# Keys and values streamed once: other pieces for the keys, other places for the weights

## The chip, the cores and the metric

The kernel runs on one core of one Trainium2 chip. The metric is the device time of one execution in microseconds (us). Before the change the median of three runs is 664.82 us (663.97 to 667.68). TensorE is called PE, VectorE DVE, ScalarE ACT, GpSimd POOL; SyncE (SP) here only issues DMAs, which run on the core's sixteen DMA engines.

## The reference

One decoding step of a transformer block, four sequences of one token each, 32 heads, 4096 cached positions, head size 128, model width 640. Attention and a gated MLP both start from the same normalised input and are added to it:

```python
q = (x @ wq).reshape(B, Sq, Hq, Dh).transpose(0, 2, 1, 3)
scores = jnp.einsum('bhqd,bhkd->bhqk', q, k) * Dh ** (-0.5)
o = jnp.einsum('bhqk,bhkd->bhqd', softmax(scores), v)
A = o.transpose(0, 2, 1, 3).reshape(B, Sq, Hq * Dh) @ wo

z = gelu(jnp.einsum('bsd,df->bsf', x, w_in))
z1, z2 = z[..., :Fh], layernorm(z[..., Fh:])
Bm = jnp.einsum('bsf,fd->bsd', z1 * (w_sp * z2 + b_sp), w_out)   # one position, so w_sp is a scalar
return x_in + A + Bm                                            # x = layernorm(x_in) in both
```

The two caches are 134 MB each in bfloat16, and every byte is used once. All else (wq, wo 5 MB each, w_in 2 MB, w_out 1 MB) is small beside them.

## The kernel before

**Units.** The work is cut into 16 units (`NU`), u = 4 * hg + b: a group `hg` of eight heads for one sequence `b`. The cached rows of a unit, 8 x 4096 of them, are laid over the 128 partitions ("lanes") so that each lane holds 256 consecutive rows: one contiguous run of 64 KB in memory for K(u), and another for V(u).

**Scores on DVE.** A K run is worked on in four quarters of 64 rows (16 KB a lane). For each quarter DVE multiplies by the query in place (`product`), adds the upper half of each row to the lower (`fold_half`), PE adds eight slices with an identity as weights (`sums`, eight matmuls into PSUM), and DVE sums the last eight values of each row (`row_sums`), one quarter later. After a unit's last quarter come `head_max`, `exps` on ACT and `by_head`, which writes the probabilities spread by head into the tile `pm` of that unit's parity. They stand inside the first quarter of the next unit. The weighted sum of V (`weighted`, 64 matmuls of PE) follows later, then a copy by ACT (`take`), and one quarter or more later a pick of the right blocks by PE (`pick_unit`, `pick_last`). At the end of a group, `group_turn` on DVE normalises and transposes and `group_proj` on PE multiplies with the group's 1.3 MB of `wo`, adding to the result in PSUM.

**Places.** SBUF holds three tiles of 32 KB a lane for K halves (`kp`, `K_SLOTS`), one of 64 KB for V (`vp`), and one of 10 KB for `wo` (`wop`). The first contents of the V tile are wq and w_in (`w_a`), of the `wo` tile w_out (`w_b`).

**Order of loads.** All large loads are issued by SP, in the order of the list `loads`: K halves 0 to 2, then for each unit its V and the next two K halves (three after units 3, 6, 9: `EXTRA_K`), then the last two units' V as four halves in K's places and V's. SP's queue is strictly in order: a load that waits for its place holds up all that stand behind it. `pump` lets loads into the program as soon as the user of their place is written down. The loop over the 32 halves is written out by hand (`manual_schedule`), so each engine keeps exactly that order. `turns` says after which half a V run's weighted sum stands. `gmlp`, the whole gated MLP, stands ahead of the loop.

Of the kernel before, what the change touches and what calls it, by code (L numbers as in the profile page):

```python
# [9 lines left out]
FP32 = mybir.dt.float32  # L10
# [4 lines left out]

K_SLOTS = 3
EXTRA_K = (3, 6, 9)
# [3 lines left out]
def kernel(  # L21
# [36 lines left out]
    NC = NR // 2  # L58
    HC = NC // 2
    NT = 2 * NU  # L60
    HD2 = Dh // 2
    RW = 8
    SLOT = NC * Dh
# [12 lines left out]
    kp = ctx.enter_context(tc.tile_pool(name="kp", bufs=K_SLOTS))  # L76
    vp = ctx.enter_context(tc.tile_pool(name="vp", bufs=1))
    wop = ctx.enter_context(tc.tile_pool(name="wop", bufs=1))
# [14 lines left out]

    w_a = vp.tile([P, 2 * SLOT], BF16, tag="v", name="w_a")
    wq_sb = w_a[:, 0 : DC * HD].rearrange("p (c n) -> p c n", c=DC)
    w_in_sb = w_a[:, DC * HD : DC * (HD + F)].rearrange("p (c n) -> p c n", c=DC)
    w_b = wop.tile([P, HT, D], BF16, tag="wo", name="w_b")
    w_out_sb = w_b[:, 0:NFC, :]
# [7 lines left out]
    nc.sync.dma_start(out=w_in_sb, in_=B_w_in.rearrange("(p c) n -> p c n", c=DC))  # L106
    nc.sync.dma_start(
        out=w_out_sb[:, 0:NFF, :], in_=B_w_out[0 : NFF * P].rearrange("(p k) n -> p k n", k=NFF)
    )
    nc.sync.dma_start(out=w_out_sb[:FT, NFF, :], in_=B_w_out[NFF * P : Fh])  # L110
# [7 lines left out]
    k_tiles, v_tiles = {}, {}  # L118
    V_CUTS = (0, 64, 96, 112, NC)

    def half_run(t, cache, i, cuts=(0, NC)):
        u, half = divmod(i, 2)
        for c0, c1 in zip(cuts, cuts[1:]):
            nc.sync.dma_start(
                out=t[:, c0 * Dh : c1 * Dh],
                in_=run_of(cache, u)[:, (half * NC + c0) * Dh : (half * NC + c1) * Dh],
            )
        return t[:, 0:SLOT].rearrange("p (c d) -> p c d", d=Dh)

    def load(which, n):  # L130
        if which == "k":
            k_tiles[n] = half_run(kp.tile([P, SLOT], BF16, tag="k", name="k_nat"), A_k_cache, n)
        elif which == "v":
            t = vp.tile([P, 2 * SLOT], BF16, tag="v", name="v_nat")
            nc.sync.dma_start(out=t[:], in_=run_of(A_v_cache, n))  # L135
            v_tiles[n] = t[:].rearrange("p (c d) -> p c d", d=Dh)
        elif which == "h":
            v_tiles["h", n] = half_run(
                kp.tile([P, SLOT], BF16, tag="k", name="v_half"), A_v_cache, n
            )  # L140
        else:
            t = vp.tile([P, 2 * SLOT], BF16, tag="v", name="v_end")[:, 0:SLOT]
            v_tiles["h", n] = half_run(t, A_v_cache, n, V_CUTS)

    loads = [("k", 0), ("k", 1), ("k", 2)]
    n_k = 3
    turns = {}
    for u in range(NU - 2):
        turns[n_k - 1] = u
        loads.append(("v", u))  # L150
        for _ in range(3 if u in EXTRA_K else 2):
            if n_k < NT:
                loads.append(("k", n_k))
                n_k += 1
    loads += [("h", NT - 4), ("h", NT - 3), ("h", NT - 2), ("e", NT - 1)]
    used = set()
    n_loaded = [0]
    holders = {"k": [], "v": [("w", 0)]}

    def pump():  # L160
        while n_loaded[0] < len(loads):
            which, n = loads[n_loaded[0]]
            ring, slots = (holders["v"], 1) if which in "ve" else (holders["k"], K_SLOTS)
            if len(ring) >= slots and ring[-slots] not in used:
                return
            load(which, n)
            ring.append((which, n))
            n_loaded[0] += 1

    wo_tiles = {}  # L170

    def load_wo(hg):
        wo_tiles[hg] = wop.tile([P, HT, D], BF16, tag="wo", name="wo")
        rows = A_wo[hg * HT * Dh : (hg + 1) * HT * Dh]
        if hg == HG - 1:
            by_head = rows.rearrange("(h p) n -> p h n", p=P)
            for h0, h1 in ((0, 2), (2, 4), (4, 6), (6, 7), (7, 8)):
                nc.sync.dma_start(out=wo_tiles[hg][:, h0:h1, :], in_=by_head[:, h0:h1, :])
            return
        nc.sync.dma_start(  # L180
            out=wo_tiles[hg][:].rearrange("p (e j) n -> p e j n", e=PAR),
            in_=rows.rearrange("(e p j) n -> p e j n", e=PAR, j=JR),
        )
# [20 lines left out]
    p_m = [const.tile([P, NG, CB, HT], BF16, name=f"pm{n}") for n in range(2)]  # L204
# [121 lines left out]
    def gmlp():  # L326
# [95 lines left out]
        for k in range(NFC):  # L422
            w = P if k < NFF else FT
            for half in range(2):
                nc.tensor.matmul(
                    out=out_sum(half),
                    lhsT=gm["yT"][:w, k, :],
                    rhs=w_out_sb[:w, k, half * NOH : (half + 1) * NOH],
                    start=False,
                    stop=False,  # L430
                )
# [18 lines left out]
    def half_of(i, half):  # L450
        return k_tiles[i][:, half * HC : (half + 1) * HC, :]

    def product(i, half):
        nc.vector.tensor_tensor(  # L454
            out=half_of(i, half),
            in0=half_of(i, half),
            in1=qbcs[i // 2][:, None, :].to_broadcast([P, HC, Dh]),
            op=ALU.mult,
        )

    def fold_half(i, half):
        t = half_of(i, half)
        nc.vector.tensor_tensor(  # L463
            out=t[:, :, 0:HD2], in0=t[:, :, 0:HD2], in1=t[:, :, HD2:Dh], op=ALU.add
        )

    def sums(i, half):
        t = half_of(i, half)
        s = sums_ps[i, half] = ps_s.tile([P, HC, RW], FP32, name="s_ps")
        n = HD2 // RW  # L470
        for g in range(n):
            nc.tensor.matmul(  # L472
                out=s[:],
                lhsT=ident[:],
                rhs=t[:, :, g * RW : (g + 1) * RW],
                start=(g == 0),
                stop=(g == n - 1),
            )

    def row_sums(i, half):  # L480
        u, which = divmod(i, 2)
        if (which, half) == (0, 0):
            scores[u] = small.tile([P, NR], FP32, name="s_sb")
        at = which * NC + half * HC
        nc.vector.tensor_reduce(  # L485
            out=scores[u][:, at : at + HC], in_=sums_ps.pop((i, half))[:], axis=AX.X, op=ALU.add
        )
# [25 lines left out]
    def by_head(u):  # L513
        hg, b = divmod(u, Bsz)
        nc.vector.tensor_tensor(  # L515
            out=p_m[u % 2][:],
# [16 lines left out]
    def weighted(u, v_at, g0=0, more=False):  # L533
# [3 lines left out]
        for n in range(n_g):  # L537
# [3 lines left out]
                lhsT=p_m[u % 2][:, g0 + n].rearrange("p c h -> p (c h)"),  # L541
# [55 lines left out]
    def group_proj(hg):  # L597
        for n, o in enumerate(gr.pop(hg)):
            for half in range(2):
# [3 lines left out]
                    rhs=wo_tiles[hg][:, n, half * NOH : (half + 1) * NOH],  # L603
                    start=False,
                    stop=(hg == HG - 1 and n == HT - 1),
                )

# [18 lines left out]

    E = mybir.EngineType
    with tc.manual_schedule(engines={E.PE, E.DVE, E.Activation, E.SP}):
        stage_q(0)
        gmlp()  # L630
        used.add(("w", 0))
        pump()
        for i in range(NT):
            u, half = divmod(i, 2)
            due, done = turns.get(i), turns.get(i - 1)
            closed = None
            if done is not None and done % Bsz == Bsz - 1 and done // Bsz < HG - 1:
                closed = done // Bsz
            product(i, 0)
            if i:  # L640
                row_sums(i - 1, 1)
            if half == 0 and u:
                head_max(u - 1)
            if done is not None:
                picked(done)
            fold_half(i, 0)
            if half == 0 and u:
                exps(u - 1)
                by_head(u - 1)
            sums(i, 0)  # L650
            if closed is not None:
                group_turn(closed)
            if half == 0 and u + 1 < NU:
                stage_q(u + 1)
            product(i, 1)
            row_sums(i, 0)
            fold_half(i, 1)
            sums(i, 1)
            if closed is not None:
                group_proj(closed)  # L660
            if due is not None:
                if due % Bsz == Bsz - 1:
                    group_den(due // Bsz)
                weighted(due, v_tiles[due])
                take(due)
                used.add(("v", due))
            used.add(("k", i))
            pump()
            if i % (2 * Bsz) == 6 and i // (2 * Bsz) < HG - 1:
                load_wo(i // (2 * Bsz))  # L670
        load_wo(HG - 1)
        row_sums(NT - 1, 1)
# [3 lines left out]
        picked(NU - 3)  # L676
# [10 lines left out]
        weighted(NU - 2, v_tiles["h", NT - 4], more=True)  # L687
        weighted(NU - 2, v_tiles["h", NT - 3], NG // 2)
        take(NU - 2)
        for n in (NT - 4, NT - 3):  # L690
            used.add(("h", n))
        picked(NU - 2)
        u, b = NU - 1, Bsz - 1
        weighted(u, v_tiles["h", NT - 2])
        take(u)
        pick_last(u, more=True)
        for c in range(NC):
            nc.tensor.matmul(  # L698
                out=o_last[0][:, :, :, b],
                lhsT=v_tiles["h", NT - 1][:, c, :],  # L700
                rhs=p_m[u % 2][:, NG // 2 + c // CB, c % CB, :].rearrange("p (e k) -> p k e", e=PAR),
# [43 lines left out]
```

## Time and profile before

| | |
|---|---|
| median of three runs | 664.82 us |
| the profiled execution's own time | 663.56 us |
| its span, first to last instruction | 661.8 us |
| bytes loaded | 282.24 MB, 426 GB/s over the span |
| DVE busy | 522.4 us (79%) |
| PE busy | 328.9 us (50%) |
| ACT busy | 29.7 us (4%) |

A row of a group of instructions gives its line, engine and operation, what it writes and reads, the count, the busy time and the mean in ns. "Idle before" is time in which the engine stood still ahead of these, with what released it. Matmuls are pipelined, so a matmul's duration is longer than its share of a series: eight of `sums` take 3.57 us together, though one is shown with 0.6. A DMA's "time to landing" runs from its issue on SP to the semaphore that says it has arrived, and so holds the time that it stands in the queue behind earlier loads. The DMA share is the mean busy share of the sixteen DMA engines in a stretch.

### The profile page before, as it was taken

Reading aid. Unit: us, or ns where it says so; the run is one execution under the profiler, and the core shown is the slowest. Engines: PE = TensorE matmul, PEld = TensorE weight load, DVE = VectorE, ACT = ScalarE, POOL = GpSimd, SP = SyncE. Lnnn points to the kernel's source line nnn. Section 1 sums busy time; section 2 is a strip of 40 time slices with the busy share of each in tenths; the row PEclk is TensorE's granted clock in tenths of the full one; section 3 lists DMA queues with packets and bytes.
Section 4 is the critical chain, followed back from the end, with each engine's and each line's share of the span. In section 5 each row is a group of like instructions: output and inputs, shape, how many; then the busy total and the mean of one; then the engine's idle time right before and its main releaser. Section 6 shows DMA issues by size and latency. Waiting matters only on the chain.

```text
span 661.8 us, 4641 instructions
## 1 busy us (share of the span) xinstructions
PE 328.9 (50%) x1999; PEld 131.6 (20%) x1999; DVE 522.4 (79%) x325; ACT 29.7 (4%) x73; POOL 2.7 (0%) x12
## 2 busy tenths in 40 slices
PE   0625363645454555454635354644446455354656
PEld 0311121212121112121211121212112122121223
DVE  2399899695969998959599899696996978969600
ACT  0200000000000000000000000000000000000000
POOL 1000000000000000000000000000000000000000
PEclk9767686767756678577755686777566557776866
DMA  9999999999999999999999999999999999999996
GB/s 368 432 442 434 422 443 420 453 420 422 451 406 446 460 402 455 418 442 436 423 431 436 426 435 424 460 412 425 452 407 448 458 404 453 414 443 440 418 424 278
DMA packets 10144, 282.54 MB, mean 427 GB/s; under 512 B 1056, under 2 KB 2188, under 8 KB 3340
## 3 DMA queue, kind: packets, MB, share of 16 engines
q1 hardware_dynamic: 10104, 282.25, 99.1%
q8 instruction: 15, 0.25, 0.1%
q14 instruction: 5, 0.04, 0.0%
q10 hardware_dynamic: 20, 0.01, 0.0%
HBM read 282.24 MB, written 0.01 MB: 426 GB/s over the span
## 4 chain that ended last, share of the span: by engine, by line
DMA 50%; DVE 39%; PE 9%; issue 1%; SPq 1%; ACT 0%; DVEq 0%
DMA k_nat<-in_A_k_cache_dram 42%; DVE k_nat L454 22%; DVE k_nat L463 11%; PE s_ps L472 5%; DMA v_half<-in_A_v_cache_dram 4%; PE pv L539 4%; DMA wo<-in_A_wo_dram 3%; DVE pm L515 3%; DVE s_sb L485 2%; DVE m L491 1%; DVE mt L493 0%; SPq L135 0%; DVE mt L496 0%; DVE o_n L582 0%; PE out_ps L600 0%
## 5 line engine op out<-in xcount | busy, mean ns | idle before, releaser
L472 PE MATMUL s_ps<-k_nat,ident 128*128 128x512 bf16 x512 | 219.0, 605 | 286.8 <-DVE k_nat L463 286.8
L454 DVE TENSOR_TENSOR k_nat<-k_nat,qbc 128x8192 bf16<-128x8192 bf16 x64 | 282.7, 4416 | 75.4 <-DMA k_nat<-in_A_k_cache_dram 75.4
L472 PEld LDWEIGHTS <-ident 128*128 128x128 bf16 x512 | 70.9, 138 | 417.5 <-issue 412.7
L463 DVE TENSOR_TENSOR k_nat<-k_nat 128x4096 bf16<-128x4096 bf16 x64 | 145.9, 2280 | 0.0
L539 PE MATMUL pv<-v_nat,pm 128*32 128x512 bf16 x896 | 56.2, 408 | 0.0
L485 DVE TENSOR_REDUCE s_sb<-s_ps 128x64 f32<-128x512 f32 x64 | 43.6, 681 | 3.3 <-PE s_ps L472 3.3
L515 DVE TENSOR_TENSOR pm<-p_c,own 128x2048 bf16<-128x2048 bf16 x16 | 36.6, 2284 | 2.9 <-ACT p_c L504 2.9
L539 PEld LDWEIGHTS <-pm 128*32 128x32 bf16 x992 | 27.0, 106 | 45.8 <-issue 22.1
L551 ACT COPY o_rows<-pv 128x512 f32<-128x512 f32 x16 | 9.4, 586 | 308.4 <-PE pv L539 308.4
L706 DVE TENSOR_TENSOR o_n_last<-o_last,rden_all 128x32 bf16<-128x32 f32 x1 | 0.2, 191 | 25.4 <-PE o_last L698 25.4
L570 PE MATMUL o_ps<-o_rows,pick 128*128 128x128 f32 x96 | 13.9, 288 | 8.8 <-ACT o_rows L551 8.8
L504 ACT ACTIVATE p_c<-s_sb,nm 128x256 bf16<-128x256 f32 x16 | 8.1, 508 | 197.2 <-DVE nm L498 197.2
L570 PEld LDWEIGHTS o_ps<-o_rows,pick 128*128 128x128 f32 x96 | 11.6, 191 | 14.7 <-ACT o_rows L551 14.7
L539 PE MATMUL pv<-v_half,pm 128*32 128x512 bf16 x96 | 10.6, 618 | 6.7 <-DMA v_half<-in_A_v_cache_dram 6.7
L257 DVE TENSOR_SCALAR q_rows<-q_ps 128x512 bf16<-128x512 f32 x2 | 1.4, 690 | 14.4 <-PE q_ps L249 14.4
L249 PE MATMUL q_ps<-w_a,xnT 128*32 128x512 bf16 x40 | 4.5, 630 | 11.1 <-DMA w_a<-in_A_wq_dram 11.1
L448 ACT CAST qbc<-qbc_ps 128x128 bf16<-128x128 f32 x16 | 4.3, 266 | 107.4 <-PE qbc_ps L440 107.4
L491 DVE TENSOR_REDUCE m<-s_sb 128x1 f32<-128x256 f32 x16 | 6.7, 420 | 0.6
L440 PE MATMUL qbc_ps<-q_rows,of_row 128*128 128x128 bf16 x32 | 6.3, 286 | 0.6 <-DVE q_rows L257 0.6
L440 PEld LDWEIGHTS <-of_row 128*128 128x128 bf16 x32 | 4.3, 138 | 8.6 <-issue 8.2
L616 PE MATMUL o_last<-hot,o_rows 128*128 128x8 f32 x32 | 4.2, 259 | 3.0 <-ACT o_rows L551 3.0
L616 PEld LDWEIGHTS o_last<-hot,o_rows 128*128 128x128 f32 x32 | 3.9, 191 | 5.5 <-ACT o_rows L551 5.5
(86 smaller groups left out, 70.3 us busy)
## 6 DMA issues: line engine op xcount, KB each, us to landing
k_nat<-in_A_k_cache_dram SPq DMA_DIRECT2D x32, 4096.0 KB, 33.1
v_half<-in_A_v_cache_dram SPq DMA_DIRECT2D x3, 4096.0 KB, 27.4
w_a<-in_A_wq_dram SPq DMA_DIRECT2D x1, 5120.0 KB, 15.4
wo<-in_A_wo_dram SPq DMA_DIRECT2D x3, 1280.0 KB, 35.3
w_a<-in_B_w_in_dram SPq DMA_DIRECT2D x1, 2160.0 KB
v_end<-in_A_v_cache_dram SPq DMA_DIRECT2D x1, 2048.0 KB
v_end<-in_A_v_cache_dram SPq DMA_DIRECT2D x1, 1024.0 KB
v_end<-in_A_v_cache_dram SPq DMA_DIRECT2D x2, 512.0 KB, 28.0
```

The lines of the kernel that those rows point to most:

```text
L440: nc.tensor.matmul(out=qb_ps[:], lhsT=of_row[:, e, b].rearrange("p k f l -> p (k f l)"), rhs=q_rows[e][:, hg, :], start=(e == 0), stop=(e ...
L454: nc.vector.tensor_tensor(out=half_of(i, half), in0=half_of(i, half), in1=qbcs[i // 2][:, None, :].to_broadcast([P, HC, Dh]), op=ALU.mult,)
L463: nc.vector.tensor_tensor(out=t[:, :, 0:HD2], in0=t[:, :, 0:HD2], in1=t[:, :, HD2:Dh], op=ALU.add)
L472: nc.tensor.matmul(out=s[:], lhsT=ident[:], rhs=t[:, :, g * RW : (g + 1) * RW], start=(g == 0), stop=(g == n - 1),)
L485: nc.vector.tensor_reduce(out=scores[u][:, at : at + HC], in_=sums_ps.pop((i, half))[:], axis=AX.X, op=ALU.add)
L491: nc.vector.tensor_reduce(out=m1[:], in_=scores[u][:], axis=AX.X, op=ALU.max)
L504: nc.scalar.activation(out=p_c[u][:], in_=scores.pop(u)[:], func=ACT.Exp, bias=maxes.pop(u)[:], scale=1.0, accum_out=row_den[hg % NACC][:, ...
L515: nc.vector.tensor_tensor(out=p_m[u % 2][:], in0=p_c.pop(u)[:].rearrange("p (g c) -> p g c", c=CB)[:, :, :, None].to_broadcast([P, NG, CB, HT]
L539: nc.tensor.matmul(out=pvs[u][cg * QD : (cg + 1) * QD, :], lhsT=p_m[u % 2][:, g0 + n].rearrange("p c h -> p (c h)"), rhs=v_at[:, n * CB : ...
L551: nc.scalar.copy(out=o[:].rearrange("p c d -> p (c d)"), in_=pvs.pop(u)[:])
L570: nc.tensor.matmul(out=gr[hg][:], lhsT=pick[:, c, Bsz - 1 - b : P + Bsz - 1 - b], rhs=o[:, c, :], start=(b == 0 and c == 0), stop=(b == Bs ...
L616: nc.tensor.matmul(out=o_last[0][:, :, :, u % Bsz], lhsT=o[:, c, :], rhs=hot[:, c, :].rearrange("p (e k) -> p k e", e=PAR), start=(c == 0) ...
```

## The change

K(u) is loaded as one run of 64 KB a lane. K's places become one ring tile of seven quarter places of 16 KB (`k_ring`). Even units lie in places 3 to 6 and odd ones in 0 to 3, so two neighbours share place 3. The even unit has its first quarter there and the odd one its last, and the odd unit works on that quarter first (`k_order`). So K(u+2) may be issued when all of unit u and the first quarter of unit u+1 are done, that is, one unit ahead. Units 0, 14 and 15 are loaded in halves, the last two into other places. V's tile stays; V(14) is now loaded into it as one run, and V(15) in two parts into places 0 to 3.

`wo` has no tile of its own any more: each group's lies in place 6, the last quarter of an even unit, and its load stands in the one list, behind the K that follows the group's last V. Place 6 is given back by `group_proj`, now one quarter after `group_turn`. w_out is loaded into the probabilities' tile (`p_m`, one tile for both parities), its last 96 rows into V's tile behind w_in. The first half of K(0) is loaded ahead of w_in and w_out, and `gmlp` stands after the second quarter of the loop instead of ahead of it. The loop runs over 64 quarters.

```diff
-K_SLOTS = 3
-EXTRA_K = (3, 6, 9)
...
+    NK = 4
+    HC = NR // NK
+    NC = 2 * HC
...
+    QW = HC * Dh
+    RING = 2 * NK - 1
...
+    ring = places.tile([P, RING, QW], BF16, name="k_ring")
+    v_all = places.tile([P, NK * QW], BF16, name="v_all")
+    p_m = const.tile([P, 2, NG, CB, HT], BF16, name="p_m")
...
+    k_at, k_order = {}, {}
+    for u in range(NU):
+        k_at[u] = [r if u % 2 else NK - 1 + r for r in range(NK)]
+        k_order[u] = [NK - 1, 0, 1, 2] if u % 2 else [0, 1, 2, 3]
+    k_at[NU - 2], k_order[NU - 2] = [4, 5, 0, 1], [0, 1, 2, 3]
+    k_at[NU - 1], k_order[NU - 1] = [2, 3, 4, 5], [0, 1, 2, 3]
+    VE_AT, WO_AT = (0, 2), 6
+
+    def k_load(u, r0=0, r1=NK):
+        at = k_at[u][r0:r1]
+
+        def go():
             nc.sync.dma_start(
+                out=ring[:, at[0] : at[0] + r1 - r0, :],
+                in_=run_of(A_k_cache, u)[:, r0 * QW : r1 * QW].rearrange("p (r w) -> p r w", w=QW),
             )
+
+        return go, at
...
-    loads = [("k", 0), ("k", 1), ("k", 2)]
...
-    for u in range(NU - 2):
-        turns[n_k - 1] = u
-        loads.append(("v", u))
-        for _ in range(3 if u in EXTRA_K else 2):
-            if n_k < NT:
-                loads.append(("k", n_k))
-                n_k += 1
-    loads += [("h", NT - 4), ("h", NT - 3), ("h", NT - 2), ("e", NT - 1)]
+    loads = [k_load(0, 0, 2), (load_w, []), k_load(0, 2, 4), k_load(1)]
+    for u in range(NU - 4):
+        loads += [v_load(u), k_load(u + 2)]
+        if u % Bsz == Bsz - 1:
+            loads.append(wo_load(u // Bsz))
+    assert u + 2 == NU - 3
+    loads += [k_load(NU - 2, 0, 2), v_load(NU - 4), k_load(NU - 2, 2, 4), k_load(NU - 1, 0, 2)]
+    loads += [v_load(NU - 3), k_load(NU - 1, 2, 4), v_load(NU - 2)]
+    loads += [ve_load(0, (0, NC)), ve_load(1, V_CUTS), wo_load(HG - 1)]
+    busy = {V}
...
     def pump():
         while n_loaded[0] < len(loads):
+            go, at = loads[n_loaded[0]]
+            if busy.intersection(at):
                 return
+            go()
+            busy.update(at)
             n_loaded[0] += 1
...
+    turns = {NK * (u + 1) + 2: u for u in range(NU - 4)}
+    turns[NK * (NU - 3) + 3] = NU - 4
+    turns[NK * (NU - 2) + 3] = NU - 3
...
+        for n in range(NK * NU):
+            u, i = divmod(n, NK)
+            product(n)
+            if n:
+                row_sums(n - 1)
+            if i == 0 and u:
                 head_max(u - 1)
+                if waiting is not None:
+                    picked(waiting)
+                    if waiting % Bsz == Bsz - 1 and waiting // Bsz < HG - 1:
+                        closed = waiting // Bsz
+                    waiting = None
+            fold_half(n)
+            if i == 0 and u:
                 exps(u - 1)
                 by_head(u - 1)
+            sums(n)
             if closed is not None:
+                if i == 0:
+                    group_turn(closed)
+                else:
+                    group_proj(closed)
+                    closed = None
+            if i == 0 and u + 1 < NU:
                 stage_q(u + 1)
+            if n == 1:
+                gmlp()
+                busy.remove(V)
+            if n in turns:
+                w = waiting = turns[n]
+                if w % Bsz == Bsz - 1:
+                    group_den(w // Bsz)
+                weighted(w, v_runs)
+                take(w)
+                busy.remove(V)
             pump()
```

`sums(n)` gives back its quarter's place (`busy.remove(k_at[u][r])`) and `group_proj` place 6 (`busy.remove(WO_AT)`). Behind the loop, the last two units' weighted sums and the last group's projection stand as before.

## The prediction

> **What bounds the kernel now.** I read the page from the top first: which engine is full, in every slice.
>
> ```profile
> span 661.8 us, 4641 instructions
> PE 328.9 (50%) x1999; PEld 131.6 (20%) x1999; DVE 522.4 (79%) x325; ACT 29.7 (4%) x73; POOL 2.7 (0%) x12
> DMA  9999999999999999999999999999999999999996
> q1 hardware_dynamic: 10104, 282.25, 99.1%
> ```
>
> No engine is full, but the sixteen DMA engines are: the load queue's packets fill 99.1% of the span. Then the busy time by stretch (the last two columns are DMA share and GB/s), to see whether that holds inside the loop:
>
> ```profile
> 34.00:110.00 76.00, 35.76 (x150) 13.17 (x151) 72.63 (x37) 3.87 (x9) 0.00 (x0) 0.66 1.00 433
> 110.00:300.00 190.00, 96.17 (x543) 37.00 (x543) 158.00 (x89) 7.00 (x19) 0.00 (x0) 0.68 1.00 433
> 300.00:600.00 300.00, 150.68 (x816) 58.29 (x815) 259.76 (x146) 11.05 (x31) 0.00 (x0) 0.66 1.00 433
> ```
>
> The share is 1.00 and the rate 433 GB/s everywhere, at the group ends too. So a 64 KB run a lane (8.39 MB) takes 19.4 us, half of it 9.7, a unit (K and V) 38.75. The chain of waits names DVE for 39% of the span, but only because it follows a load back to the work that freed its place; the load then stood in a queue. How long, the issues with their time to landing show (last column, median us):
>
> ```profile
> k_nat<-in_A_k_cache_dram SPq DMA_DIRECT2D x32, 4096.0 KB, 33.1
> v_nat<-in_A_v_cache_dram SPq DMA_DIRECT2D x14, 26.4
> wo<-in_A_wo_dram SPq DMA_DIRECT2D x3, 1280.0 KB, 35.3
> ```
>
> A K half is issued 33.1 - 9.7 = 23.4 us before its own transfer begins, a V run 26.4 - 19.4 = 7.0 us (22.7 - 19.4 = 3.3 for the shortest landing of a V tile). This lead is what the change can spend: while it is positive nothing else matters; when it is negative, every microsecond is added to the end. To price it I need the pace of DVE and PE within a unit, from the chain in order of time and from the timeline at a group's end:
>
> ```profile
> 136.06 4.33 DVE k_nat L454
> 140.40 0.61 DVE s_sb L485
> ...
> 141.03 0.43 DVE m L491
> ...
> 142.14 2.20 DVE k_nat L463
> 144.34 2.20 DVE pm L515
> 146.54 4.33 DVE k_nat L454
> ...
> 153.73 3.57 PE s_ps L472 x8
> ```
>
> ```profile
> 206.51 0.77 DVE L582 TENSOR_SCALAR o_n<-o_ps,rden 128x128 bf16<-128x128 f32 x1
> 207.31 0.31 DVE L590 STREAM_TRANSPOSE o_t<-o_n 128x128 bf16<-128x128 bf16 x1
> 214.78 3.57 PE L472 MATMUL s_ps<-k_nat,ident 128*128 128x512 bf16 x8 [4.83 <-DVE k_nat L463]
> 218.28 1.45 PE L600 MATMUL out_ps<-wo,o_t 128*4 128x320 bf16 x16
> 218.38 0.33 SPq L124 DMA_DIRECT2D k_nat<-in_A_k_cache_dram  x1
> ```
>
> A quarter costs DVE 4.33 + 0.60 + 2.20 = 7.13 us, the first of a unit 10.48 (136.06 to 146.54, softmax of the unit before included), a unit 31.87; it fits into 38.75. The sums of a quarter take PE 3.57 us, the weighted sum of a V run 3.6 to 4.6, a group's projection 1.4 (until 219.73), its turn on DVE 1.2 (206.3 to 207.55).
>
> **The change, part by part.** Every engine keeps its instructions (DVE 325), but SP issues 52 DMAs instead of 66.
>
> *Longer runs.* 13 units' K come as one DMA. Gain: GB/s over share in pure K stretches is 433/1.01 (25 to 50 us) and 434/1.01 (113 to 128), in V stretches 445/1.03 (55 to 69) and 454/1.05 (95 to 108): 429 to 432, 0.6%. On 13 x 8.39 MB (252 us) that is 1.5 us; shares have two digits, so 0 to -2.5. I take -1.0. The V rows exclude a loss: such runs already go at full rate.
>
> The fixed part of each issue is hidden in these rows: three K halves issued together land 9.7 us apart. The Trainium skill ("DMA: Bandwidth & Descriptors", the two cost components under the anatomy of one DMA) prices a DMA at about 2.0 us plus bytes at 436 GB/s, so 14 fewer would be worth 28 us; the share of 1.00 disagrees.
>
> *Steady units.* Count from the landing of K(u+1), with V(u)'s transfer just begun. K(u+2) needs all of unit u and the first quarter of u+1, the shared place: 4.33 + 0.61 + 1.04 (maximum) + 2.20, then 3.57 of sums: issued at 11.8; its turn is at 19.4. V(u+1) needs the third quarter, then weighted(u): 10.48 + 2 x 7.13 + 3.57 + 4.4 = 32.7; its turn is at 38.75. From issue to first data on an empty queue I take 1.0 us, as at the start (first issue at 0.74, no data in the first microsecond, 456 GB/s in the second), the nearest row, as it too is a long load; the upper end is 2.5, what the small last write takes in all (issued at 659.29, span's end 661.8). Leads of 6.6 and 5.0: cost nothing. They replace leads of 23 and 7, so what stands behind SP's waits counts now.
>
> *wo in place 6.* wo(0) stands on SP's queue ahead of V(4), and waits for the last quarter of unit 4, the last user of place 6: 31.87 on DVE; then PE has weighted(3) (until 33) and the sums (1.9 warm to 3.57), so 35 to 36.9, with 1.0 to data 38 at most, against 38.75. V(4) is still in time: nothing, up to 1 us if late.
>
> K(6) is not. It needs place 6 back, so it waits for the projection that reads wo, one quarter after the group's turn. From the landing of K(5): 10.48 + 1.2 (turn) + 7.13 + 3.57 + 1.4 + 0.1 (semaphore, issue) + 1.0 = 24.9 us. Ahead of it lie only wo and V(4): 3.5 + 19.4 = 22.9 (wo's 1280-byte pieces run at some 380 GB/s, as in the tail's 383 and 404). The queue is dry for 2.0 us; if the engines end apart, their mean waits longer: in the last three microseconds of loads the share is 0.87, 0.55, 0.26, so the mean ends 1.3 us before the last: 3.3. I take 2.7. It happens after groups 0 and 1: 5.4. After group 2 nothing waits for place 6, as units 14 and 15 do not use it. DVE cannot give it back: the lost time is DMA time.
>
> The page of the Trainium skill named above speaks against the change here: with its fixed 2.0 us where I have 1.0, each dry spell would be 1 us longer, an estimate of 7.4 for both.
>
> *The front.* K(0)'s first half now lands at 16.1 (wq) + 9.7 = 26 instead of 34.5; that gains nothing, the bytes ahead of the end are the same. gmlp now stands between quarters 1 and 2: PE 3.5 and DVE's chain 6.0 (25.1 to 31.1), during which DVE works on nothing else. Quarter 4 starts at 67, 4 us after K(1) lands (16.1 + 9.7 + 8 of weights + 9.7 + 19.4 = 63). V(1) is issued at 67 + 24.7 + 3.6 + 4.4 = 100, with data at 101, against 102. Bounds 0 and +2; I take +0.3. w_out in the probabilities' tile is read long before its first writer: nothing.
>
> *The tail.* Before, V(13) was loaded after the last K; now K(15)'s second half comes after V(13). Behind the landing of K(13) stand six runs and two wo: 53 MB, 122.3 us, and 1.33 of the last projection as before: 123.6. DVE and PE need in that time: three units and a turn, 95.6 + 1.2; twice 0.9, as exp now stands behind the copy of a weighted sum on ACT; from the last fold to weighted(14) 9 to 11 (618.8 to 629.8 before, 2 of it that copy); weighted(14) 3.6 warm to 7.2 cold; half of V(15) 1.8 to 3.6; two copies and picks of 1.7; the last 128 matmuls 4.0; normalising and projection 3.1. Sum 123.5 to 130.9: 0 to +7 over the loads. PE comes almost straight from sums and warms up (64 took 4.4 from cold sums at 83.9), so near the low end: +1.5. This cover did not matter before.
>
> **Sum:** -1.0 + 0 + 5.4 + 0.3 + 1.5 = +6.2. The profiled execution took 663.56 (span 661.8 and 1.8 around it): 669.8. It is 1.26 under the median of the three runs (664.82), so against that median: 671.0.
>
> **Rivals.**
> - *No dry spell (not slower).* Between cold and warm PE lie 1.7 us for eight sums (3.57 at 214.78, 1.89 at 387.41). If quarter 5's sums run warm, K(6)'s chain is 23.2 and the spell 0.3; with a covered tail -1.0 + 0.6 + 0.3 = 0: 664.7. It decides when the chain from K(5)'s landing to issue comes under 21.9. Against it: PE is idle for 3.5 us before those sums, and cold there in the rows above. 0.14.
> - *More waits of the same kind.* wo's own issue late (+1 each), a restart of 2 us, within its bounds (+1 each), the front +2, the tail +5 cold: -1 + 2 x (3.3 + 2) + 2 + 5 = 16.6 at most, 681; half of these extras gives 676. For it: PE's granted clock of 0.66 to 0.68. Against: steady leads of 5 us absorb each alone. 0.21.
> - *Fewer issues pay (faster).* If each of the 14 issues left a gap, the share could hide 0.5% of 566 us, 2.8 us over some 45 transfers: 0.9 us for 14; with -2.5 for runs, no dry spells and a covered tail, 661.4. The skill's 2.0 us each, above, would make it 637. Against it: the share, and a K(6) that must wait. 0.03.
>
> **How the numbers follow.** The likeliest (0.62) is 671, with its own range 667.5 to 674.5. Down to 666.5 leaves out most of the first and third rival, up to 677.5 a quarter of the second: 0.2 in all. A measurement of this kernel can tell about 0.5%, 3.3 us. Slower by more: nearly all of the likeliest and all of the second, 0.81. Within: the first and the low edge of the likeliest, 0.16. Faster: 0.03.
>
> **What would show it.** Two dips of the DMA share, at about 240 and 400 us, of 2 to 4 us each, just before K issues released by the projection; K issues of 64 KB a lane landing about 26 us after issue (19.4 and the lead of 6.6); DVE waiting for K 5 to 8 us in every unit; the last loads ending about 4 to 6 us later. I am wrong if the share stays 1.00 through both group ends, if dips come in every unit (then a steady lead is mis-sized), or if the loads end in time and the end still moves (then it is the tail).

## The result and the profile after

The changed kernel takes 679.27 us (median of six runs, 678.63 to 680.39) beside 663.75 us for the kernel before on the same chip. The ratio is 1.0226, with a 95% interval from 1.0203 to 1.0249: slower by 2.3%. The forecast was 671.0 with a range that ended at 677.5, so the direction was right and the size was not: the change costs about 15.5 us, where 6.2 had been worked out. Of the four executions of the first try with the MLP moved forward, two (688.07 and 698.82 us) fell into a slower state of the chip and are left out of its ratio below.

The profiled execution took 679.59 us, its span is 677.8 us. These are the lines of the page that answer to those of before, with the group of the scores' products added (last columns: busy time and mean ns, then the idle time before them and what ended it):

```profile
span 677.8 us, 4614 instructions
PE 303.5 (45%) x1999; PEld 128.0 (19%) x1999; DVE 522.5 (77%) x325; ACT 29.6 (4%) x73; POOL 2.7 (0%) x12
DMA  9999999999999979999999989999999999999995
q1 hardware_dynamic: 8088, 282.24, 97.3%
L481 DVE TENSOR_TENSOR k_ring<-k_ring,qbc 128x8192 bf16<-128x8192 bf16 x64 | 282.7, 4417 | 98.1 <-DMA k_ring<-in_A_k_cache_dram 98.1
```

DVE's work is unchanged to a tenth of a microsecond (522.4 before). What changed is the row of the DMA engines: it is no longer full in two slices inside the loop. Each slice is 16.9 us, so the 7 stands at 237 to 254 us and the 8 at 390 to 407; the last slice, where the loads end, is a 5 and was a 6. The queue's share times the span gives the time that the packets took: 97.3% of 677.8 is 659.5 us, against 99.1% of 661.8, 655.8. So of the 16.0 us that the span grew, 12.3 are time in which the DMA engines had nothing to do, and 3.7 are packets that took longer. The same bytes moved.

The busy time by stretch, for the same three stretches as before (last two columns: DMA share and GB/s), says how much of it lies inside the loop:

```profile
34.00:110.00 76.00, 37.16 (x226) 16.33 (x224) 62.16 (x54) 6.88 (x13) 0.00 (x0) 0.59 1.00 427
110.00:300.00 190.00, 86.23 (x540) 35.48 (x540) 153.58 (x83) 6.67 (x18) 0.00 (x0) 0.68 0.98 422
300.00:600.00 300.00, 130.07 (x801) 54.09 (x801) 244.34 (x139) 10.94 (x31) 0.00 (x0) 0.68 0.99 424
```

Where it was 433 GB/s throughout, each stretch now has less. The first loses 6 of 433 with a full share, so its packets were slower. Now the end of the first group in fine steps, same columns. A packet is counted where it starts, and one of 64 KB takes some 2.4 us, so short steps scatter, but three microseconds without data are a gap:

```profile
236.00:241.00 5.00, 1.43 (x4) 0.55 (x4) 5.00 (x4) 0.00 (x0) 0.00 (x0) 0.53 0.97 419
241.00:244.00 3.00, 3.00 (x20) 1.06 (x19) 3.00 (x2) 0.00 (x0) 0.00 (x0) 0.64 0.00 0
244.00:246.00 2.00, 0.35 (x6) 0.10 (x1) 2.00 (x2) 0.00 (x0) 0.00 (x0) 1.00 1.55 524
```

The chain of waits in order of time (start, us, what) names the work that filled this gap:

```profile
193.90 26.54 DMA k_ring<-in_A_k_cache_dram
220.53 4.42 DVE k_ring L481
...
228.91 2.20 DVE p_m L542
231.29 0.78 DVE o_n L609
...
239.57 3.57 PE s_ps L496 x8
243.14 1.23 PE out_ps L627 x16
244.38 21.82 DMA k_ring<-in_A_k_cache_dram
...
357.51 26.49 DMA k_ring<-in_A_k_cache_dram
...
406.70 1.37 PE out_ps L627 x16
408.08 22.93 DMA k_ring<-in_A_k_cache_dram
```

K(5) lands at 193.90 + 26.54 = 220.44. DVE then does the first quarter, the turn of the group and the second quarter, PE the sums and the projection (L627), and K(6) is issued at 244.38: 23.94 us after the landing. K(10), likewise, is issued at 408.08, 24.1 after the landing of K(9) at 384.0. No such step stands in the chain after the third group.

How the queue starts again, the stretch from 243 to 246 us shows in 40 steps of 0.075 us (its rate, then its packets, MB and share):

```profile
GB/s 0 0 0 0 0 0 0 0 0 0 0 0 0 0 0 0 0 0 0 0 0 0 0 0 0 0 0 0 0 0 0 4369 2621 1748 874 1748 874 874 0 874
q1 hardware_dynamic: 16, 1.05, 103.1%
```

The first data comes in the 32nd step, at 245.3, 1.0 us after K(6)'s issue. Sixteen packets of 64 KB start, one for each engine; together they take 103.1% of 16 x 3 us, so 3.1 us each, where such a packet takes 2.42 in a full queue. The trace gives the other end, too: the engines had finished V(4) one by one between 241.1 and 242.8, at 241.5 in the mean, and its landing was told at 243.07. So an engine stood still for 4.0 us in the mean, of which the late issue is 1.3 (243.07 to 244.38). At K(10) it was 3.5 us, with 0.7 of late issue.

The issues of the load queue, with their median time to landing, show the steady units:

```profile
k_ring<-in_A_k_cache_dram SPq DMA_DIRECT2D x13, 26.7
v_all<-in_A_v_cache_dram SPq DMA_DIRECT2D x15, 26.2
```

19.4 us of a K's 26.7 are its own transfer, so it is issued 7.3 us before its turn ("turn" is the landing of the load ahead, and "lead" the time from an issue to it).

Last, the tail, in the timeline (start, us, engine and line, operation; in brackets the idle time before it and its releaser):

```profile
618.91 5.16 PE L566 MATMUL pv<-v_all,p_m 128*32 128x512 bf16 x64 [2.43 <-DMA v_all<-in_A_v_cache_dram]
624.17 0.59 ACT L578 COPY o_rows<-pv 128x512 f32<-128x512 f32 x1 [32.23 <-PE pv L566]
624.66 0.51 ACT L531 ACTIVATE p_c<-s_sb,nm 128x256 bf16<-128x256 f32 x1
625.29 2.29 DVE L542 TENSOR_TENSOR p_m<-p_c,own 128x2048 bf16<-128x2048 bf16 x1 [4.16 <-ACT p_c L531]
...
657.39 0.63 PE L705 MATMUL den_all<-acc,ones_sq 128*128 128x32 f32 x2 [5.05 <-DVE acc L551]
657.95 6.11 PE L566 MATMUL pv<-v_all,p_m 128*32 128x512 bf16 x64
```

The weighted sum of unit 13 waits for V(13) to land and then takes 5.16 us; ACT copies its result before it computes the probabilities of unit 14, and DVE stands still for 4.16 us. From here to the end, the chain runs on DVE and PE, with short pieces of ACT, and no longer on loads. In it the weighted sum of unit 14 takes 6.11 us, after PE had stood idle for 5.05.

**Where the 16.0 us are.** The landings in the trace split them. A load that is never late lands 19.3 us after the one ahead (a half 9.65, `wo` 3.05).

| | later by, us |
|---|---|
| K(6): lands at 266.20, V(4) ahead of it at 243.07; 23.1 | 3.8 |
| V(5) behind it: lands at 287.21; 21.0 | 1.7 |
| K(10): lands at 431.01, V(8) ahead of it at 407.38; 23.6 | 4.3 |
| front: K(2), then V(1) (82.36, 102.92, 123.76; 20.6 and 20.8) | 1.3 + 1.5 |
| second half of K(14) | 0.8 |
| `wo` of the first two groups, issued 3.5 and 3.3 us before their turn (3.2 and 3.8) | 0.9 |
| K(1) | 0.4 |
| all other loads, less the 3.8 us by which loads came late in the kernel before | -2.0 |
| last load to the end of the span: 3.4 before, 6.7 after | 3.3 |
| sum | 16.0 |

V(5) was issued 12.4 us before its turn and is late all the same. It belongs to the spell: the engines, which had ended V(4) 1.7 us apart, restart together and end K(6) 0.6 us apart, and by V(5) the slowest is 1.8 us behind the first again. V(5) is 1.0 to 1.7 us late in each of the five profiles with a spell at K(6), and in time in the kernels below that have none. So the two spells cost 5.5 and 4.3 us (5.54 and 4.34), 9.9 together.

### The profile page after: what moved, and what is told of

The parts are those of the page before. It is cut to its first block, busy times and chain, and to the rows that moved or that the text cites. A ratio compares the mean times of both kernels' runs of the same rounds, so it can differ in the third digit from the quotient of the medians.

```text
span 677.8 us, 4614 instructions
## 1 busy us (share of the span) xinstructions
PE 303.5 (45%) x1999; PEld 128.0 (19%) x1999; DVE 522.5 (77%) x325; ACT 29.6 (4%) x73; POOL 2.7 (0%) x12
## 3 DMA queue, kind: packets, MB, share of 16 engines
q1 hardware_dynamic: 8088, 282.24, 97.3%
## 4 chain that ended last, share of the span: by engine, by line
DMA 54%; DVE 31%; PE 13%; issue 1%; ACT 1%; SPq 0%; DVEq 0%; ACTq 0%
DMA k_ring<-in_A_k_cache_dram 50%; DVE k_ring L481 16%; DVE k_ring L487 8%; PE s_ps L496 8%; DMA v_all<-in_A_v_cache_dram 5%; PE pv L566 2%; DVE s_sb L509 2%; DVE p_m L542 2%; DVE m L518 1%; PE out_ps L627 1%; PE zT L355 1%; PE o_last L722 0%; DVE mt L520 0%; DVE mt L523 0%; DVE nm L525 0%
## 5 line engine op out<-in xcount | busy, mean ns | idle before, releaser
L481 DVE TENSOR_TENSOR k_ring<-k_ring,qbc 128x8192 bf16<-128x8192 bf16 x64 | 282.7, 4417 | 98.1 <-DMA k_ring<-in_A_k_cache_dram 98.1
L496 PE MATMUL s_ps<-k_ring,ident 128*128 128x512 bf16 x512 | 199.9, 561 | 339.6 <-DVE k_ring L487 339.3
L496 PEld LDWEIGHTS <-ident 128*128 128x128 bf16 x512 | 65.9, 130 | 453.5 <-issue 379.5
L487 DVE TENSOR_TENSOR k_ring<-k_ring 128x4096 bf16<-128x4096 bf16 x64 | 145.9, 2280 | 0.0
L566 PE MATMUL pv<-v_all,p_m 128*32 128x512 bf16 x960 | 62.8, 421 | 2.4 <-DMA v_all<-in_A_v_cache_dram 2.4
L542 DVE TENSOR_TENSOR p_m<-p_c,own 128x2048 bf16<-128x2048 bf16 x16 | 36.6, 2286 | 5.2 <-ACT p_c L531 5.2
L566 PEld LDWEIGHTS <-p_m 128*32 128x32 bf16 x992 | 26.7, 105 | 41.4 <-issue 21.6
L730 DVE TENSOR_TENSOR o_n_last<-o_last,rden_all 128x32 bf16<-128x32 f32 x1 | 0.2, 193 | 14.3 <-PE o_last L722 14.3
L270 PE MATMUL q_ps<-v_all,xnT 128*32 128x512 bf16 x40 | 4.5, 630 | 10.4 <-DMA v_all<-in_A_wq_dram 10.4
## 6 DMA issues: line engine op xcount, KB each, us to landing
k_ring<-in_A_k_cache_dram SPq DMA_DIRECT2D x6, 4096.0 KB, 20.6
```

Of the source, the lines that this page charges most:

```text
L481: nc.vector.tensor_tensor(out=t, in0=t, in1=qbcs[u][:, None, :].to_broadcast([P, HC, Dh]), op=ALU.mult)
L487: nc.vector.tensor_tensor(out=t[:, :, 0:HD2], in0=t[:, :, 0:HD2], in1=t[:, :, HD2:Dh], op=ALU.add)
L496: nc.tensor.matmul(out=s[:], lhsT=ident[:], rhs=t[:, :, g * RW : (g + 1) * RW], start=(g == 0), stop=(g == m - 1),)
L542: nc.vector.tensor_tensor(out=p_m[:, u % 2], in0=p_c.pop(u)[:].rearrange("p (g c) -> p g c", c=CB)[:, :, :, None].to_broadcast([P, NG, CB, HT]
L566: nc.tensor.matmul(out=pvs[u][cg * QD : (cg + 1) * QD, :], lhsT=p_m[:, u % 2, g0 + n].rearrange("p c h -> p (c h)"), rhs=v_at[:, n * CB : ...
```

## The experiments

Each is an edit of the changed kernel. Four parts of the working were open to doubt: the projection's place (the dry spells), ACT's order (the tail), the place of the MLP (the front), and the length of the K runs.

**The projection directly behind the turn.** K(6) then waits one quarter less, and nothing else in the order moves.

```diff
-                if i == 0:
-                    group_turn(closed)
-                else:
-                    group_proj(closed)
-                    closed = None
+                group_turn(closed)
+                group_proj(closed)
+                closed = None
```

> The group's projection moves one quarter earlier, right behind the turn on DVE, so place 6 is free 7.1 us sooner. Theory A (the time went into two dry spells of the load queue, K(6) and K(10) issued too late behind the projection; 4.3 and 3.8 us idle, and the first packets after them 0.7 us slower each): both vanish, the changed kernel's 679.3 falls by 8 to 10 us to about 670. Rival B (the queue is too short everywhere, or long K runs are themselves slower, and the spells only show where it surfaces): the time is lost elsewhere, 676 or more.

Measured: 672.40 us (671.71 to 674.02), ratio 1.0107 [1.0071, 1.0143]. K(6) is now issued at 234.94, some 9 us before its turn, and the same three microseconds are filled:

```profile
241.00:244.00 3.00, 2.92 (x7) 0.88 (x6) 3.00 (x1) 0.00 (x0) 0.00 (x0) 0.50 0.91 393
```

V(4) and K(6), and V(8) and K(10), land 19.3 us apart. So the two spells are the projection's, and without them the time falls by about 7 us (by the ratios to the kernel before 7.9, as the two kernels were not measured beside each other). The loads' end does not carry through in full, though: they are through at 664.0, 7.1 sooner, but the span ends 8.2 us behind them, and the chain that ended last is the tail of DVE and PE (lines in order of time):

```profile
579.02 32.28 DMA v_all<-in_A_v_cache_dram
611.34 6.15 PE pv L566 x64
...
618.05 0.61 ACT p_c L531 x2
...
651.69 6.42 PE pv L566 x64
```

**The projection one quarter later.** The opposite dose: `group_proj` stands behind the third quarter.

```diff
-                else:
+                elif i == 2:
                     group_proj(closed)
                     closed = None
```

> The other direction: the projection one quarter later than in the changed kernel. Theory A: each of the two spells grows by one quarter of DVE, 7.1 us, so about 679.3 + 14 = 693.5. Rival B: the spells are not what sets the end, within 3 us of 679.

Measured: 694.76 us (692.41 to 696.52), ratio 1.0428 [1.0382, 1.0474]; 15.5 us above the changed kernel (13.4 by the ratios). One quarter is 7.13 us on DVE; two group ends make 14.3. The chain shows the issues at 251.37 and 421.89, where they were at 244.38 and 408.08:

```profile
250.15 0.91 PE out_ps L627 x12
251.37 21.81 DMA k_ring<-in_A_k_cache_dram
...
420.68 0.91 PE out_ps L627 x12
421.89 22.20 DMA k_ring<-in_A_k_cache_dram
```

The first is 6.99 later, the second 13.81, the sum of two delays. Once K is late, further delay comes out at the end in full, to within what the two measurements can tell, and DVE does not give it back. That is the law that the prediction used.

**ACT's copy behind the probabilities.** For units 12 and 13 alone, the copy of the weighted sum (with its pick) moves behind `exps`.

```diff
-                if waiting is not None:
+                if waiting is not None and waiting < NU - 4:
                     picked(waiting)
...
                 by_head(u - 1)
+                if waiting is not None:
+                    take(waiting)
+                    picked(waiting)
+                    waiting = None
...
-                take(w)
+                if w < NU - 4:
+                    take(w)
```

> For the last two units whose copy by ACT stands ahead of the exponentials of the unit after, the copy moves behind them; nothing else. Theory C (the tail is set by DVE and PE, which lost 4.2 us at 621 to 625 because the exponential stood behind a copy that waited for V(13)): DVE goes on, the end comes 3 to 4 us sooner, about 675.8, and then the last loads set it again. Rival D (the tail hangs on PE's cold weighted sums or on the loads): under 1 us, 678.5 or more.

Measured: 677.28 us (675.13 to 677.9), ratio 1.0171 [1.0133, 1.0209]. That is 2.0 us under the changed kernel's median (by the ratios 3.6; the intervals just touch). The profile is clearer than the time: DVE's idle time ahead of `by_head`'s products goes from 5.2 to 0.7 us over the kernel, and the end of the chain now consists of loads:

```profile
625.25 24.29 DMA v_all<-in_A_v_cache_dram
...
649.55 22.42 DMA k_ring<-in_A_wo_dram
...
672.01 1.25 PE out_ps L627 x8
```

The wait in the tail was ACT's order. From the last load to the end it is now 3.3 us, as in the kernel before (3.4), instead of 6.7.

**The first matmuls of the MLP one quarter earlier.** The 70 matmuls on w_in stand after the first quarter, the rest of the MLP after the second, as it was. (`gmlp` is split in two for this; only the calls are shown.)

```diff
+            if n == 0:
+                gmlp_in()
             if n == 1:
                 gmlp()
```

> The first matmuls of the gated MLP move one quarter earlier, so that DVE does not stand still for them. Theory E (DVE comes 4 us late to K(1), which makes K(2) and V(1) late: 0.8 us of idle queue and some 1.1 us of slow first packets): 1 to 2 us sooner, about 677.7. Rival: the leads of the first units cover it, no change beyond 0.5 us.

The ratio is 1.0187 [1.0132, 1.0241], from two times (678.75 and 677.09): too little to read. The same kernel again, beside the changed kernel on one chip:

> The gated MLP's first matmuls a quarter earlier, once more, as the profile of the first try was of a disturbed run. Theory E: K(2) and V(1), which were issued 3.2 and 3.3 us before the load ahead of them landed and came 1.2 and 1.5 us late, get 6 us more of lead, so they land 19.3 to 19.4 us after the load before, and the time is 2 to 3 us under the changed kernel's in this call. Rival: within 0.7 us of it.

> The changed kernel once more on the chip of these two, so that they can be set against it: 679 to 680 or a ratio of 1.020 to 1.025 to the kernel before.

Measured: 678.40 us (676.11 to 680.7), ratio 1.0158 [1.0086, 1.0230], against 680.35 us (679.09 to 681.33), ratio 1.0188 [1.0106, 1.0271], for the changed kernel. K(2) is issued at 75.31 and V(1) at 95.53, 4 us earlier than in the first profile (79.21 and 99.65). Both now land 19.3 us after the load ahead, so the 2.8 us of late landings are gone; the time moves by 2.0, within what four runs each can tell. That the late issues are the MLP's doing is shown; what they cost the whole is not settled.

**All three together, and unit 13 in memory order.** The three edits, and the last odd unit worked on in the order of its places, so that the places of K(14)'s second half come free earlier.

```diff
+    k_order[NU - 3] = [0, 1, 2, 3]
```

> The changed kernel with the projection in the turn's quarter, the last two copies behind the exponentials, the gated MLP's first matmuls a quarter earlier, and unit 13 worked on in memory order (its places 0 and 1, which the first half of K(14)'s successor waits for, come free a quarter sooner). Theory A: all that the change lost were issues too late for the queue and the uncovered tail; with leads of several us everywhere the loads end at about 658 to 659 as before, the tail is within 2 us of them, and the time is 664 to 666, a ratio of 0.999 to 1.004 to the kernel before. Rival B (something in the ring or in long runs is slower in itself): 668 or more.

Measured: 666.11 us (664.91 to 667.97, twelve runs) against 664.14 of the kernel before, ratio 1.0015 [0.9987, 1.0043]. The loss is gone to within what can be told. The page's DMA row and the load queue's share of the span:

```profile
DMA  9999999999999999999999999999999999999996
q1 hardware_dynamic: 8088, 282.24, 98.8%
```

98.8% of 664.0 is 656.0 us of packets, as before the change (655.8). So nearly all of the 3.7 us by which packets had become slower went with the late issues, too: they were not a price of the longer runs or of the ring's places.

**The same, with each K run as two loads of 32 KB a lane.** This puts the 13 issues back that the change had saved.

```diff
-            nc.sync.dma_start(
-                out=ring[:, at[0] : at[0] + r1 - r0, :],
-                in_=run_of(A_k_cache, u)[:, r0 * QW : r1 * QW].rearrange("p (r w) -> p r w", w=QW),
-            )
+            for h0 in range(r0, r1, 2):
+                nc.sync.dma_start(
+                    out=ring[:, at[h0 - r0] : at[h0 - r0] + 2, :],
+                    in_=run_of(A_k_cache, u)[:, h0 * QW : (h0 + 2) * QW].rearrange(
+                        "p (r w) -> p r w", w=QW
+                    ),
+                )
```

> The same kernel, but each K run issued as two DMAs of 32 KB a lane, one right behind the other, into the same places. What the longer runs are worth by themselves: if only the pieces' length counts, 1.0 us or less (0 to 2.5) slower than all4; if each issue costs a fixed 2 us, 26 us slower.

Measured: 664.22 us (663.32 to 668.24, twelve runs), ratio 0.9999 [0.9980, 1.0019]. So the long runs gain nothing. The halves are 1.9 us quicker, and though the two intervals overlap, ten of their twelve times lie below the lowest of the whole runs (664.91). The Trainium skill ("DMA: Bandwidth & Descriptors", the two cost components under the anatomy of one DMA) gives a fixed part of about 2.0 us for one DMA, measured there on DMAs that GpSimd issues. If each of these 13 issues paid it in the stream, that would be 26 us, an estimate; issued by SP behind a filled queue, the runs show no such price. No version here is faster than the kernel before.

**Only the halves.** The changed kernel, projection and tail and front as they were, but K as two loads of 32 KB. If a spell comes from the projection's place alone, it stays; if it comes from one load that waits for the last of its four places, it goes.

> The changed kernel, with its order, its ring and its wo in place 6 as they are; only each K run is issued as two DMAs of 32 KB a lane. The first half of K(6) then waits only for places 3 and 4, free after the first quarter of unit 5, 11.8 us after K(5) lands, and only its second half waits for the projection, with 9.7 us of transfer ahead of it. Theory A (the two dry spells come from one DMA waiting for the last of its four places): they vanish although the projection is as late as ever, about 8 us less than the changed kernel, 670 to 673. Rival (the spells come from the projection's place in the order, and the length of a K run has no part in them): 678 or more.

Measured: 670.17 us (667.62 to 675.05, ten runs), ratio 1.0072 [1.0043, 1.0101]; 10.2 us under the changed kernel on the same chip. The same stretch of the group's end, and the two issues of K(6), which the timeline puts in one line, the first at 231.74 and the second 12 us later:

```profile
241.00:244.00 3.00, 2.70 (x20) 0.91 (x18) 3.00 (x3) 0.00 (x0) 0.00 (x0) 0.72 0.96 415
```

```profile
231.74 12.32 SPq L139 DMA_DIRECT2D k_ring<-in_A_k_cache_dram  x2
```

The projection is as late as ever, and the second half still waits for it. But the first half needs only places that came free a quarter earlier, and its 9.7 us of transfer cover the wait. The dry spells come from the two things together: a load as large as four places, and one place that comes back late. V(4), K(6), V(8) and K(10) land in time, as does V(5). The 10.2 us are what the two spells cost, with the load behind each (10.0 us in the changed kernel's profile from this chip). Of the 4.9 us that remain against the kernel before, about 3 are the tail, whose chain again ends on DVE and PE (6.4 us from the last load to the end, where it was 3.4); the rest was not split further.

Not tried: a tile of its own for `wo` beside the ring.

## Why the prediction was right or wrong

**The bound: right; the law of the lead: right below zero, too lenient above.** The DMA queue bounds both kernels, and time lost in it is not recovered; the projection one quarter later cost 15.5 us (13.4 by the ratios) for 14.3 of delay. But "while it is positive nothing else matters" does not hold down to zero: leads of 3.1 and 3.3 us cost 1.3 and 1.5 in the front.

**The spells: right place and chain, wrong price.** "From the landing of K(5): ... = 24.9 us" with 1.0 of it from issue to data, so 23.9 to the issue; measured 23.94 and 24.1. wo and V(4) were to last 22.9 us; they landed 22.6 and 23.4 after K(5) and K(9). Nothing happened after the third group. So the issue came 1.0 us behind the last landing in the mean of both, just as worked out, and the first data 1.0 us (0.96 and 0.97) after the issue. But the spells cost 5.5 and 4.3 us, 9.9 together, where 5.4 was taken and 6.6 was the upper end.

The step that failed is the price that stands behind these two terms: "if the engines end apart, their mean waits longer ... 3.3. I take 2.7." It was short in two ways. The engines' ends apart were worked out as 1.3 us, from the end of the loads before, and then only 0.7 of it was taken; measured, the mean engine ends 1.5 and 1.6 us ahead of the landing. And a restart has a part that the sum put at nothing: the first packets take 3.1 us instead of 2.42, 0.7 more. With late issue, first data, engines and slow packets the spells come to 4.7 and 4.2 us in the mean of the engines (4.0 and 3.5 of standing still, 0.7 of slow packets); the rest, up to 5.5 and 4.3, is the slowest engine, which shows in the landing of V(5).

The estimate that the prediction made with the 2.0 us of the Trainium skill ("DMA: Bandwidth & Descriptors", the two cost components under the anatomy of one DMA), 7.4 for both, lies nearer to 9.9, but not because the first data came later: it came 1.0 us after the issue, as the kernel's start had shown.

A reading was wrong without effect: `wo` was priced at 3.5 us, by the rate of the small pieces in the tail. The groups' `wo` moves in packets of 5120 bytes, not 1280, and took 3.1 us in the kernel before; being issued late, it came to 3.2 and 3.8 here.

**The front: wrong by the same step.** The predicted issue of V(1) at 100 was right (99.65), and so was its turn at 102 (K(2) landed at 102.9). Data one microsecond before the turn counted as enough. But the turn is the slowest engine's: the first engines were done at 100.3, and V(1)'s first packets were slow, 2.5 to 3.5 us. K(2) and V(1), with leads of 3.1 and 3.3 us, came 1.3 and 1.5 late, so 2.8 in place of +0.3, and above the bound of +2. The second half of K(14) was issued 4.0 us ahead of its turn and came 0.8 late; nothing was in the sum for it.

**The steady units and wo(0): right.** Leads of 6.6 and 5.0 cost nothing, as forecast; K's time to landing was put at about 26 us and is 26.7, DVE's waits for K at 5 to 8 us a unit and are 98.1 us in 13 waits, 7.5 each. V(4) behind wo landed in time; wo itself came 0.2 and 0.7 late, inside its bound of 1.

**Longer runs: wrong.** -1.0 was taken from shares with two digits. Whole runs against halves, with all else covered, are 666.11 against 664.22: no gain, rather a loss, whose cause is open.

**The tail: right that its cover was gone, short in size.** +1.5 was taken, +3.3 measured. The term is "twice 0.9, as exp now stands behind the copy of a weighted sum on ACT". It counted the copy, not what the copy itself waits for: unit 13's weighted sum, which waits for V(13)'s landing and then runs 5.16 us. One wait of 4.16 us takes the place of 0.9. The copy moved behind the probabilities gave 2.0 us or more back. "PE comes almost straight from sums and warms up" was wrong, too: the weighted sum of unit 14 came after 5.05 us of idle PE and took 6.11 us, near the 7.2 of its cold end and not the 3.6 of its warm one.

**Of the rivals,** the second, more waits of the same kind, came nearest: 676 with half of its extras and 681 with all, against 679.27. Spells of up to 5.3 each, a front of +2 and a tail of up to +5 were its parts, and each was needed in some measure; the spells were as long as it said, though the first data did not take the 2 us that it named. Nearly all stood in the working as upper ends of terms, and the sum had taken a value near the low end of most, though the spells and the front share one cause, a load issued too close to its turn. Of the terms forecast at 5.4 + 0.3 + 0 + 1.5 = 7.2, 9.9 + 2.8 + 0.8 + 3.3 = 16.8 were measured; the remaining -0.8 to the span's +16.0 are the last rows of the table's loads.

**Left open:** why halves are a little quicker than whole runs; why the first packets after a gap are slow; the separate effect of unit 13's order; how much of the front's 2.8 us reaches the end.

## What to carry to other kernels

In a stream that keeps the DMA engines full, a load may be made larger only if the last of its places comes free early enough: a merged load waits for its latest place, a split one starts in the earliest. Count the lead of each load to the landing of the load ahead, and ask for some 5 us of it, not for more than zero. A load that comes after the queue ran dry is priced by more than its delay and its first byte: add what the engines' uneven ends and the first slow packets cost. Where the loads no longer end last, read which result the in-order engines of the tail must copy before the one that others wait for.

## What the runs showed of the hardware that was not expected

**A queue that ran dry costs its delay and some 3.7 us more.** Five profiles hold two spells each (the changed kernel twice, the projection later, the copy moved, the MLP moved). K(6) or K(10) was issued 0.4 to 8.7 us after the landing of the load ahead, and together with the load behind it landed late by that delay and 3.6 to 4.2 us more (2.9 in one of the ten). In all ten the first data came 0.96 or 0.97 us after the issue, the mean engine had ended the load ahead 1.3 to 2.4 us before its landing, and the first packets of 64 KB took 3.0 to 3.1 us in the mean, where 2.42 is the median. Why they do is not shown by any run.

**A lead of a few microseconds is not enough.** Over the K and V runs of ten profiles, those issued 2.5 to 4 us before the landing of the load ahead came 1.1 us late in the mean (18 loads, 0 to 2.2), those with 4 to 4.5 us 0.3. From 4.5 us up it is 0.1 in the mean of 352 loads, and does not depend on the lead; single ones are up to 1.7 late, V(5) behind a spell among them; for the others no run shows why. The sixteen engines end one load mostly 1.5 to 2.8 us apart, at most 3.8.

**64 KB a lane is no faster than 32 KB** at 433 GB/s, and 13 issues more cost nothing (664.22 us with them, 666.11 without), so long as the queue is never empty.
